# The table of the first two batches in another order: v-weight conversions ahead of the first state

## The chip, the cores and the metric

The kernel runs on one core of a Trainium2 chip. The time is the device time of one execution in microseconds (us); the number that counts is the median over several runs. The engines are TensorE (PE; its weight loads PEld), VectorE (DVE), ScalarE (ACT), GpSimd (POOL) and SyncE (SP), which here issues every transfer between HBM and the on-chip memory SBUF. Matmul results lie in PSUM banks.

## What is computed

Eight batches of 576 positions go through an attention with decay (eight heads of 64) and then through a gated block with a spatial mixing. Cut to what matters:

```python
scores = (q @ k.T) / sqrt(64)                      # per batch and head
x = (scores * gamma[h] ** (i - j) for i >= j) @ v  # heads side by side: 512 wide
h = maximum(x @ w_in, 0)                           # 512 -> 1024
u, v = h[..., :512], h[..., 512:]
v_n = (v - mean(v)) / sqrt(var(v) + 1e-6)
v_s = w_spatial @ v_n + b_spatial[:, None]         # over the 576 positions
out = (u * v_s) @ w_out                            # 512 -> 512
```

All inputs and outputs are 32-bit floats. A product of two of them is made of three products of halves (a high part, rounded, and the low rest), so each weight is converted once into such a pair before its first use.

## The kernel before

Each batch's positions are four chunks of 128 and a tail of 64. The attention is computed with a running state: a chunk needs its scores within itself (`scores_chain`, line 625: products of q and k, then a mask on VectorE into tile at), the state's update (`state_chain`, line 631: products of the scaled k and of v into PSUM; then sh, a decay in dec, and the next state st), and a burst of products with the state and with v (`burst_chain`, line 648). In the burst a tiny copy on ScalarE (`turned`, line 538: r<-warm) stands between the two halves; at its end ScalarE casts the chunk's result into slot (high part) and VectorE subtracts (low part). Before the update, k is scaled by the decay terms (`prep_k`, line 464, eight steps on ScalarE or one on another engine).

Weights come as 64-bit words and are converted by `weight` (line 394) in seven steps: absolute value (ScalarE), a clamp, two to three bit operations (VectorE), a cast to the high part (ScalarE), and a subtraction for the low part. Kind 1 are the v halves of w_in, in four blocks; kind 0 the u halves; kind 2 is w_out. `spatial` (line 418) splits w_spatial. `v_chain` (line 682) makes and normalizes v, `vs_chain` and `g_chain` the spatial mixing, `gated_chain` the gate, `f_chain` and `product_chain` the output. From batch 2 on the products go by a scheme with fewer products, and the weights' sums for it are made in between (`made_weight`, line 336).

The order of all this is written out by hand. Each entry of the tables ORDER (line 43), STEADY and LAST names a generator and advances it by one step; all engines issue in the program's order:

```python
for name in order.split():
    ...
    chain = chains.get(name)
    if chain is None:
        chain = chains[name] = makers[head](*rest)
    next(chain)
```

ORDER covers batches 0 and 1 and the start of batch 2 and 3, once. STEADY then runs for batches 2 to 5, and LAST for 6 and 7. The letters: d loads a chunk (its q and k, its k in the other layout, its v), D a weight block, S w_spatial, T a tail, c the constants (c.a is fixed_terms). g are scores, p the state, b the burst, q and k the scalings; w is a weight's conversion (w.1.3.vp is v block 3 with the clamp on VectorE and the subtraction on GpSimd), s the spatial split, v the v chain, U, V, G, P the first batch's gate, y and X the later gate, A the made weights, F and W output products, R, K, Y, Z their operands. An entry z is one dummy product (`spin`, line 230) of 128x512 that reads a zeroed part of wsp and whose result nobody reads; there are 43. BANKS (line 151) says which of the four PSUM banks m0 to m3 each use of a bank takes, in the order of use.

Buffers are shared: chunks 2 and 3 of batch 0 are loaded into tiles that are later u and wout0 (in the profile u and lent_wout), the four v blocks and later w_spatial into the tile of slot1 (lent_slot), the other weights into raw. Helpers record every operation at line 204, so all rows of the profile have this line.

Of the kernel before, what the change touches and what calls it, by code (L numbers as in the profile page):

```python
# [18 lines left out]
P = 128  # L19
B, H, S, D = 8, 8, 576, 64  # L20
# [28 lines left out]
    z.34.1 z.35.1 w.1.0.vp z.18.1 w.1.3.vp b.0.1 S z.4.1 b.0.1 w.1.3.vp w.1.0.vp z.8.1 p.0.1.aa b.0.1 S w.1.3.vp
    w.1.0.vp b.0.1 w.1.2.pp z.31.1 b.0.1 z.9.1 w.1.3.vp z.29.1 c.t z.37.1 k.0.2.a q.0.2.p z.38.1 w.1.2.pp g.0.2  # L50
    b.0.1 d.1.0 z.6.1 w.1.1.vp w.1.2.pp z.7.1 p.0.1.aa d.1.0 p.0.2.aa z.0.1 w.0.0.vp p.0.2.aa z.12.1 v.0.0 w.1.3.vp
    w.1.2.pp w.0.0.vp p.0.2.aa z.14.1 w.1.2.pp g.0.2 b.0.2 w.0.0.vp z.36.1 w.1.3.vp S v.0.1 w.0.1.vp p.0.2.aa
    w.1.3.vp w.0.0.vp v.0.0 k.0.3.a S w.0.1.vp v.0.0 m w.0.0.vp v.0.0 w.0.1.vp D.2.0 q.0.3.p b.0.2 v.0.0 d.1.0
    p.0.2.aa d.1.1 v.0.0 t.0.p t.0.p b.0.2 b.0.2 g.0.3 S w.0.2.pp p.0.3.ap w.0.1.vp s.1.p t.0.p z.28.1 w.0.2.pp
    p.0.3.ap v.0.1 b.0.2 g.0.3 p.0.3.ap v.0.1 b.0.2 q.1.0.p v.0.1 d.1.1 s.0.p p.0.3.ap s.1.p w.0.2.pp b.0.3 d.1.1
    g.1.0 w.0.1.vp b.0.3 v.0.1 b.0.3 k.1.0.p g.1.0 v.0.0 v.0.2 v.0.0 s.2.p v.0.2 s.0.p v.0.1 s.3.p b.0.3 w.0.0.vp
    w.0.2.pp s.2.p p.1.0.pp e.0.v T.1 v.0.0 v.0.2 e.0.v D.2.1 w.0.2.pp b.0.3 d.1.2 s.3.p v.0.2 v.0.1 D.0.3 b.0.3
    v.0.3 d.1.2 v.0.0 v.0.2 w.0.0.vp v.0.3 p.1.0.pp v.0.1 v.0.4 s.4.p v.0.2 v.0.4 p.1.0.pp w.0.2.pp v.0.4 k.1.1.p
    e.0.v v.0.3 v.0.1 v.0.2 v.0.1 b.1.0 s.4.p v.0.3 b.1.0 p.1.0.pp v.0.2 v.0.4 v.0.3 q.1.1.p U.1 v.0.4 w.0.1.vp
    v.0.4 s.5.p p.1.0.pp v.0.3 g.1.1 v.0.4 s.5.p b.1.0 U.1 b.1.0 v.0.4 d.1.3 v.0.2 p.1.1.pp d.1.2 v.0.2 U.0 w.0.1.vp  # L60
    b.1.0 v.0.4 p.1.1.pp b.1.0 p.1.1.pp v.0.4 V.0.0 w.0.2.pp U.0 V.0.0 v.0.3 g.1.1 V.0.0 v.1.0 v.0.3 w.2.0.vv
    k.1.2.p v.0.4 v.1.0 p.1.1.pp w.2.0.vv v.0.4 t.1.p v.1.0 v.0.3 v.0.4 p.1.1.pp v.1.0 v.0.3 q.1.2.p b.1.1 w.2.0.vv
    g.1.2 b.1.1 w.2.1.vp p.1.2.pa w.2.0.vv d.2.0 v.1.0 b.1.1 b.1.1 d.1.3 w.2.1.vp w.0.3.pv w.2.0.vv d.2.0 V.0.0
# [971 lines left out]
```

## Time and profile before

| what | value |
|---|---|
| median of 3 runs | 509.9 us (509.21 to 511.1) |
| span of the profiled execution | 506.5 us |
| TensorE busy (matmuls) | 498.4 us, 98% |
| TensorE weight loads | 472.6 us, 93% |
| VectorE, ScalarE, GpSimd busy | 395.2, 259.3, 152.1 us |

The profiled execution is one run; what the runs' time has beyond its span lies around the program. A row of the timeline gives the start and the length of one or several equal instructions, in brackets how long the engine was idle ahead of it and what ended that. The windows give each engine's busy time in a stretch and, as PEclk, the share of TensorE's full clock that was granted in it. The chain that ended last goes from step to step back to what released it. Dummy products count as busy.

### The profile page before, as it was taken

The numbers are of one execution on the slowest core, as the hardware profiler recorded it, in microseconds if no ns is written. First come the engines' busy times: TensorE is split into PE (matmuls) and PEld (weight loads), VectorE is DVE, ScalarE is ACT, GpSimd is POOL, SyncE is SP. The second block draws the span as 40 slices with busy tenths as digits, with TensorE's granted clock in tenths as the row PEclk, the third lists the DMA queues.
The fourth block names the chain that finished last, engine by engine and source line by source line (L and its number), as shares of the span: only waits on it lengthen the run. The fifth ranks groups of instructions, "written<-read, shape, count | busy, mean of one in ns | idle before, by whom it ended". The sixth has DMA issues, their size and how long they took to land.

```text
span 506.5 us, 17036 instructions
## 1 busy us (share of the span) xinstructions
PE 498.4 (98%) x7335; PEld 472.6 (93%) x7335; DVE 395.2 (78%) x881; ACT 259.3 (51%) x587; POOL 152.1 (30%) x133
## 2 busy tenths in 40 slices
PE   7999999999999999999999999999999999999997
PEld 5778999999999999999999999999999999999996
DVE  3798898768789886788669786888867886788756
ACT  2798544645344652537336472446525574357513
POOL 1499633314127430345014250243303240020000
PEclk8999999999999999999999999999999999999999
DMA  8987522025515422152222441054221520011002
GB/s 295 407 294 243 167 74 82 2 68 146 167 55 167 158 65 84 45 187 85 63 85 90 143 148 62 24 152 161 67 86 45 182 90 1 1 41 54 2 1 93
DMA packets 29516, 55.52 MB, mean 110 GB/s; under 512 B 2945, under 2 KB 15361, under 8 KB 29186
## 3 DMA queue, kind: packets, MB, share of 16 engines
q1 hardware_dynamic: 29442, 54.45, 32.8%
q8 instruction: 57, 0.93, 0.8%
q14 instruction: 17, 0.14, 0.1%
HBM read 45.00 MB, written 9.44 MB: 107 GB/s over the span
## 4 chain that ended last, share of the span: by engine, by line
PE 91%; DVE 4%; ACT 2%; DMA 1%; issue 0%; SPq 0%; DVEq 0%; ACTq 0%
PE m L204 78%; PE r L204 14%; DVE u L204 2%; DMA fixed_terms<-in_terms 1%; DVE slot L204 1%; ACT slot L204 1%; DVE kn L204 1%; ACT dec L204 0%; ACT u L204 0%; ACT lent_wout L204 0%; DVE x L204 0%; ACT f L204 0%; ACT win L204 0%; DVE at L204 0%; SPq L204 0%
## 5 line engine op out<-in xcount | busy, mean ns | idle before, releaser
L204 PE MATMUL m<-wsp,vn 128*128 128x288 f32 x768 | 113.0, 296 | 0.0
L204 PEld LDWEIGHTS m<-wsp,vn 128*128 128x128 f32 x768 | 105.1, 188 | 0.6
L204 DVE TENSOR_TENSOR u<-m,u 128x288 f32<-128x288 f32 (+1 forms) x132 | 57.2, 439 | 19.1 <-PE m L204 11.6
L204 ACT COPY u<-m 128x288 f32<-128x288 f32 (+1 forms) x92 | 34.5, 384 | 38.3 <-PE m L204 30.1
L204 PE MATMUL m<-slot,win 128*128 128x288 f32 x336 | 50.5, 296 | 0.0
L204 PEld LDWEIGHTS m<-slot,win 128*128 128x128 f32 x336 | 46.5, 188 | 0.6
L204 POOL TENSOR_TENSOR slot<-u,slot 128x576 fp32r<-128x576 f32 x7 | 10.2, 1463 | 105.4 <-ACT slot L204 105.4
L204 DVE SCALAR_TENSOR_TENSOR u<-u,m 128x288 f32<-128x288 f32 x48 | 21.2, 450 | 24.8 <-PE m L204 24.6
L204 PE MATMUL m<-slot,wout 128*128 128x288 f32 x264 | 39.5, 295 | 0.4 <-issue 0.4
L204 PEld LDWEIGHTS m<-slot,wout 128*128 128x128 f32 x264 | 36.5, 188 | 0.8 <-issue 0.5
L204 PE MATMUL m<-win,slot 128*128 128x512 f32 (+1 forms) x168 | 35.3, 348 | 0.0
L204 ACT CAST slot<-u 128x576 fp32r<-128x576 f32 x32 | 21.4, 675 | 24.1 <-DVE u L204 23.8
L204 PEld LDWEIGHTS m<-win,slot 128*128 128x128 f32 x168 | 27.1, 188 | 4.2 <-DVE slot L204 0.2
L204 ACT CAST places<-u 128x576 fp32r<-128x576 f32 x21 | 14.2, 677 | 32.1 <-DVE u L204 31.8
L204 PE MATMUL m<-quarter,slot 128*128 128x256 f32 x216 | 29.7, 283 | 0.0
L204 ACT COPY r<-warm 1x2 f32<-1x2 f32 x32 | 4.9, 152 | 48.3 <-PE r L204 47.5
L204 DVE TENSOR_TENSOR at<-r,fixed_terms 128x512 f32<-128x512 f32 x32 | 21.8, 682 | 7.7 <-DMA fixed_terms<-in_terms 4.9
L204 PE MATMUL m<-slot,part 128*128 128x288 f32 x168 | 27.1, 300 | 0.4
L204 PE MATMUL m<-wtl,vt 128*128 128x288 f32 (+1 forms) x128 | 27.4, 295 | 0.0
L204 PEld LDWEIGHTS m<-quarter,slot 128*128 128x128 f32 x216 | 26.9, 188 | 0.4
L204 POOL TENSOR_TENSOR kn<-kn,fixed_terms 128x512 f32<-128x512 f32 x15 | 15.7, 1044 | 38.5 <-DMA kn<-in_qkv 29.6
L204 PE MATMUL m<-places,wout 128*128 128x288 f32 x168 | 26.8, 297 | 0.0
(166 smaller groups left out, 1210.4 us busy)
## 6 DMA issues: line engine op xcount, KB each, us to landing
qk<-in_qkv SPq DMA_DIRECT2D x30, 512.0 KB, 4.2
kn<-in_qkv SPq DMA_DIRECT2D x30, 256.0 KB, 5.0
vv<-in_qkv SPq DMA_DIRECT2D x30, 256.0 KB, 4.7
out<-u SPq DMA_DIRECT2D x28, 144.0 KB, 1.8
tail<-in_tails SPq DMA_DIRECT2D x8, 384.0 KB, 3.7
out<-o SPq DMA_DIRECT2D x18, 144.0 KB, 1.9
lent_slot<-in_w_in SPq DMA_DIRECT2D x4, 512.0 KB, 7.9
raw<-in_w_in SPq DMA_DIRECT2D x4, 512.0 KB, 10.3
```

The lines of the kernel that those rows point to most:

```text
L204: ins = op(*args, **kw)
```

## The change

Only the table ORDER and the list BANKS that goes with it are new. ORDER has the same 726 entries as before, each as often, in another order; LAST is wrapped otherwise and holds the same entries; STEADY is untouched. BANKS has other digits throughout. The head of the table:

```diff
 ORDER = """
-    d.0.0 z.40.1 c.a z.22.1 d.0.0 z.17.1 d.0.0 z.10.1 D.1.1 d.0.1 z.16.1 d.0.1 z.24.1 d.0.1 z.13.1 z.15.1 D.1.0
-    z.39.1 g.0.0 D.1.2 g.0.0 q.0.0.p D.1.3 k.0.0.v d.0.2 p.0.0.va z.19.1 p.0.0.va z.26.1 D.0.1 z.23.1 w.1.1.vp
+    c.a d.0.0 q.0.0.p d.0.0 k.0.0.v z.31.1 z.30.1 D.1.1 d.0.0 w.1.1.vp w.1.1.vp w.1.1.vp w.1.1.vp w.1.1.vp z.18.1
+    z.20.1 z.0.1 z.41.1 z.42.1 z.3.1 z.6.1 z.39.1 z.22.1 z.28.1 z.2.1 z.38.1 z.40.1 z.21.1 z.5.1 z.10.1 D.1.0 d.0.1
...
```

At the start of VectorE's program stands, before, the first chunk's mask (at), the scaling of k (kn), the decay (dec) of the state, then the conversion of the first v block (lent_vn, with its PSUM bank m) with the state's sum (st) inside:

```order
L204 TENSOR_TENSOR at_135<-r_91,fixed_terms 128x512
L204 TENSOR_TENSOR kn_95<-kn_95,fixed_terms 128x512
L204 TENSOR_TENSOR dec_79<-sh,fixed_terms 128x256
L204 TENSOR_SCALAR lent_vn_92<-lent_vn_92 128x512
L204 TENSOR_SCALAR m_87<-lent_vn_92 128x512
L204 TENSOR_TENSOR st_76<-r_91,dec_79 128x256
L204 SCALAR_TENSOR_TENSOR m_87<-lent_slot_93,m_87 128x512
L204 SCALAR_TENSOR_TENSOR lent_vn_92<-lent_slot_93,m_87 128x512
```

and now:

```order
L204 TENSOR_TENSOR kn_96<-kn_96,fixed_terms 128x512
L204 TENSOR_SCALAR lent_vn_92<-lent_vn_92 128x512
L204 TENSOR_SCALAR m_88<-lent_vn_92 128x512
L204 SCALAR_TENSOR_TENSOR m_88<-lent_slot_93,m_88 128x512
L204 SCALAR_TENSOR_TENSOR lent_vn_92<-lent_slot_93,m_88 128x512
L204 TENSOR_TENSOR at_182<-r_91,fixed_terms 128x512
L204 TENSOR_TENSOR dec_79<-sh,fixed_terms 128x256
L204 TENSOR_TENSOR st_76<-r_91,dec_79 128x256
```

The scaling of k now comes first, then four steps of the v block, and only then the mask, the decay and the state's sum.

On ScalarE, from the burst of chunk 1 to the scaling of chunk 3's k (in lent_wout), stands before (u is chunk 2's k, slot the cast of a chunk's result, win a weight's cast, f a weight's absolute value):

```order
L204 COPY r_90<-warm 1x2
L204 CAST win_66<-lent_vn_92 128x512
L204 CAST slot_217<-r_90 128x2x4x64
L204 ACTIVATE u<-u,fixed_terms 128x64 x8
L204 ACTIVATE dec_78<-st_75,fixed_terms 128x64 x4
L204 ACTIVATE f<-raw 128x512
L204 CAST win_66<-lent_vn_92 128x512
L204 ACTIVATE dec_79<-sh,fixed_terms 128x64 x4
L204 CAST win_66<-lent_vn_92 128x512
L204 ACTIVATE f<-raw 128x512
L204 ACTIVATE lent_wout_197<-lent_wout_197,fixed_terms 128x64 x8
```

and now:

```order
L204 ACTIVATE lent_vn_92<-lent_slot_93 128x512
L204 ACTIVATE dec_78<-st_75,fixed_terms 128x64 x4
L204 ACTIVATE u<-u,fixed_terms 128x64 x8
L204 CAST win_66<-lent_vn_92 128x512
L204 ACTIVATE f<-raw 128x512
L204 COPY r_90<-warm 1x2
L204 CAST win_66<-lent_vn_92 128x512
L204 ACTIVATE f<-raw 128x512
L204 CAST slot_242<-r_90 128x2x4x64
L204 ACTIVATE dec_79<-sh,fixed_terms 128x64 x4
L204 ACTIVATE lent_wout_403<-lent_wout_403,fixed_terms 128x64 x8
```

Chunk 2's scaling moved ahead of the burst's little copy, of two weight steps and of the cast of chunk 1's result; the absolute value of the last v block and a decay went ahead of it.

On TensorE, from chunk 0's update (vv_96,kn_95) to chunk 1's (vv_108,kn_107), stands before, with dummies (m<-wsp), the two halves of the burst (qsc, at) and chunk 1's scores (qk):

```order
L204 MATMUL r_91<-vv_96,kn_95 64x64 x16
L204 MATMUL m_87<-wsp_68 128x512
L204 MATMUL m_88<-wsp_68 128x512
L204 MATMUL m_89<-wsp_68 128x512
L204 MATMUL r_90<-qsc_137,sh 64x64 x4
L204 MATMUL m_86<-wsp_68 128x512
L204 MATMUL r_90<-qsc_137,sh 64x64 x4
L204 MATMUL r_90<-at_135,vv_96 64x64 x16
L204 MATMUL r_91<-qk_106 64x64 x16
L204 MATMUL m_88<-wsp_68 128x512
L204 MATMUL m_89<-wsp_68 128x512
L204 MATMUL r_91<-vv_108,kn_107 64x64 x16
```

and now, from the last but one of eighteen dummies:

```order
L204 MATMUL m_87<-wsp_68 128x512
L204 MATMUL m_89<-wsp_68 128x512
L204 MATMUL r_91<-vv_97,kn_96 64x64 x16
L204 MATMUL r_91<-qk_95 64x64 x16
L204 MATMUL r_90<-qsc_99,sh 64x64 x8
L204 MATMUL r_91<-qk_129 64x64 x16
L204 MATMUL r_90<-at_182,vv_97 64x64 x16
L204 MATMUL r_91<-vv_131,kn_130 64x64 x16
L204 MATMUL m_86<-wsp_68 128x512
L204 MATMUL m_87<-wsp_68 128x512
```

The update stands ahead of chunk 0's scores (qk_95), the dummies between the products are gone, and 22 dummies follow behind chunk 1's update, where fourteen stood; two more stand behind the first three products of the v chain.

SyncE asks for fixed_terms first, for the first v block ahead of chunk 0's v, for the second ahead of chunk 1, and for all of w_spatial behind the q, k and v of batch 1's first chunk and the q and k of its second. Block 2 of the u weights is converted later, behind the work of batch 1's third chunk, and the first gated product is that of block 2 (G.0.2) instead of block 1. The last entries X of batch 1, the operands Y and Z behind them and the first output products W stand in another order.

## Rows read from the trace of the kernel before

**Rows 1.** The page's part 1: engine, busy us, share, count.
```profile
PE 498.4 (98%) x7335; PEld 472.6 (93%) x7335; DVE 395.2 (78%) x881; ACT 259.3 (51%) x587; POOL 152.1 (30%) x133
```

**Rows 2.** Windows: stretch, length, busy us by engine, clock, DMA share, GB/s.
```profile
5.00:10.00 5.00, 3.21 (x69) 2.15 (x67) 1.77 (x4) 1.05 (x2) 0.73 (x1) 0.80 1.01 365
10.00:15.00 5.00, 5.00 (x87) 3.52 (x86) 3.39 (x6) 1.95 (x7) 2.28 (x2) 0.51 1.07 431
15.00:20.00 5.00, 5.00 (x65) 3.71 (x64) 4.01 (x8) 3.33 (x10) 1.49 (x1) 1.00 1.03 393
30.00:40.00 10.00, 10.00 (x309) 8.29 (x301) 9.06 (x22) 9.00 (x24) 10.00 (x9) 1.00 0.82 240
60.00:165.00 105.00, 104.49 (x1587) 100.22 (x1586) 85.33 (x169) 51.51 (x121) 36.71 (x27) 1.00 0.33 102
165.00:506.00 341.00, 337.48 (x4737) 327.56 (x4735) 263.60 (x612) 167.00 (x363) 76.59 (x68) 1.00 0.26 82
```

**Rows 3.** Timeline, TensorE, 0 to 22 us: start, us, operation, [idle before].
```profile
1.50 3.77 PE L204 MATMUL m<-wsp 128*128 128x512 f32 x9 [1.50 <-DVE wsp L204]
...
15.61 3.51 PE L204 MATMUL m<-wsp 128*128 128x512 f32 x14
```

**Rows 4.** Chain that ended last, whole span: start us, us, engine and tile.
```profile
21.17 0.59 ACT slot L204
21.75 1.91 ACT u L204 x8
...
24.62 0.56 ACT f L204
25.19 0.51 ACT win L204
25.70 0.97 ACT dec L204 x4
...
27.75 1.91 ACT lent_wout L204 x8
29.66 0.05 ACT r L204
...
29.75 2.10 PE r L204 x128
...
148.53 0.36 issue
```

**Rows 5.** Timeline of DMA issues, then issues by window: KB each, us to landing.
```profile
2.58 0.63 SPq L204 DMA_DIRECT2D lent_slot<-in_w_in  x1
...
7.64 0.33 SPq L204 DMA_DIRECT2D u<-in_qkv  x1
...
11.22 3.07 SPq L204 DMA_DIRECT2D lent_wout<-in_qkv  x1
...
lent_slot<-in_w_in SPq DMA_DIRECT2D x1, 512.0 KB, 6.7
...
u<-in_qkv SPq DMA_DIRECT2D x1, 1024.0 KB, 11.7
...
lent_wout<-in_qkv SPq DMA_DIRECT2D x1, 1024.0 KB, 13.3
...
lent_slot<-in_w_sp SPq DMA_DIRECT2D x4, 288.0 KB, 7.2
```

**Rows 6.** Timeline, ScalarE, 7 to 30 us, with idle time ahead and its releaser.
```profile
21.17 0.59 ACT L204 CAST slot<-r 128x512 fp32r<-128x512 f32 x1 [0.88 <-PE r L204]
```

**Rows 7.** Timeline, VectorE, 11 to 25 us.
```profile
18.92 0.69 DVE L204 SCALAR_TENSOR_TENSOR lent_vn<-lent_slot,m 128x512 int32<-128x512 int32 x1
19.52 0.42 DVE L204 TENSOR_SCALAR lent_vn<-lent_vn 128x512 f32<-128x512 f32 x1
```

**Rows 8.** Window 28 to 56 us, GpSimd alone: length, busy us, clock, DMA.
```profile
28.00:56.00 28.00, 26.97 (x26) 1.00 0.69 216
```

**Rows 9.** Timeline, TensorE, 145 to 165 us.
```profile
162.99 0.69 PE L204 MATMUL r<-vv,kn 64*64 64x64 f32 x32 [0.15 <-DVE kn L204]
```

More of the change, by code (lines that the diff above doesn't have):

```diff
@@ L49 @@
[L49 to L63, printed above, removed]
@@ new lines @@
+    d.0.1 d.0.1 D.1.2 D.1.3 d.0.2 p.0.0.va g.0.0 p.0.0.va b.0.0 w.1.0.vp b.0.0 b.0.0 g.0.0 g.0.1 b.0.0 k.0.1.p
+    p.0.0.va p.0.0.va p.0.1.aa p.0.0.va w.1.0.vp w.1.0.vp p.0.1.aa b.0.0 w.1.2.pp z.1.1 z.17.1 z.33.1 z.36.1 z.24.1
+    z.16.1 z.35.1 z.4.1 z.11.1 z.7.1 z.14.1 z.9.1 z.27.1 z.15.1 z.37.1 z.23.1 z.12.1 z.25.1 q.0.1.p w.1.2.pp
+    w.1.0.vp w.1.0.vp b.0.0 p.0.1.aa p.0.1.aa w.1.0.vp w.1.1.vp w.1.3.vp p.0.1.aa w.1.0.vp m q.0.2.p w.1.1.vp
+    w.1.2.pp g.0.1 w.1.2.pp w.1.2.pp k.0.2.a D.0.1 D.0.0 z.13.1 z.8.1 z.34.1 z.32.1 v.0.0 z.29.1 z.19.1 b.0.1
@@ new lines @@
+    w.2.2.vv G.0.3 G.1.3 e.1.v G.0.3 P.0.0.p P.0.1.p v.1.1 w.2.3.vp w.2.3.vp w.2.3.vp w.2.3.vp G.1.3 v.1.2 v.1.2
+    v.1.2 v.1.2 w.2.3.vp v.1.2 v.1.1 v.1.4 v.1.4 v.1.4 P.0.1.p P.0.0.p w.2.1.vp v.1.4 F.0.0.1 k.2.1.a A.0.12.v
+    A.0.4.v e.1.v v.1.1 v.1.2 A.0.11.v A.1.0.v p.2.0.vp v.1.2 P.1.0.v v.1.2 w.2.2.vv F.0.0.0 d.2.1 b.2.0 p.2.1.vv
+    b.2.0 F.0.0.0 F.0.0.1 v.1.4 b.2.0 b.2.0 P.1.1.v v.1.3 v.1.3 v.1.3 v.1.3 y.1.2.1 v.1.2 p.2.0.vp p.2.1.vv
+    p.2.1.vv A.0.13.v v.1.4 v.1.2 A.0.14 A.0.15.v A.1.5.p w.2.3.vp v.1.4 v.1.4 P.1.1.v v.1.3 A.1.1.v A.1.2.p
@@ L93 @@
+    K.2.7.pv q.3.0.p K.2.6.vp W.1.2.0.B W.1.2.0.B W.1.2.1.E K.2.4.vp W.1.2.1.B W.1.2.1.B K.2.4.vp K.2.5.vp
+    W.1.2.1.B p.3.0.pv p.3.0.pv K.2.5.vp W.1.2.1.B W.1.2.0.E K.2.7.pv W.1.2.0.B W.1.2.1.E K.2.4.vp
 """
@@ new lines @@
+    K.b.5.vv X.a.1.0 X.a.1.1 W.a.1.1.E Y.a.1.v K.b.7.vv X.a.1.3 X.a.1.0 X.a.0.2 X.a.1.2 X.a.1.3 Z.a.5.vv Z.a.5.vv
+    X.a.0.3 X.a.1.2 Y.a.3.v Z.a.7.vv Y.a.3.v Z.a.7.vv W.a.2.1.A X.a.0.3 Z.a.6.vv Y.a.2.v W.a.2.0.A Z.a.7.vv
+    W.a.2.0.D W.a.2.0.A Y.a.2.v W.a.2.1.A W.a.2.1.D W.a.2.0.D Z.a.5.vv W.a.2.0.C W.a.2.1.D Z.a.6.vv W.a.2.1.C
+    W.a.2.0.C R.b.2.v Z.a.6.vv W.a.2.0.B W.a.2.1.C W.a.2.0.A Z.a.4.vv W.a.2.1.A Z.a.4.vv W.a.2.0.A R.b.2.v
+    W.a.2.1.B W.a.2.1.A W.a.2.0.A Z.a.4.vv R.b.3.p W.a.2.1.A R.b.3.p W.a.2.0.A W.a.2.0.B W.a.2.1.E W.a.2.1.A
@@ new lines @@
+    W.a.2.0.B W.a.2.0.B K.b.7.vv W.a.2.1.B W.a.2.0.E K.b.6.pv W.a.2.1.B W.a.2.1.B W.b.0.0.C W.a.2.0.E W.a.2.1.E
+    W.b.0.0.A K.b.6.pv K.b.7.vv W.a.2.1.E W.a.2.0.B W.b.0.1.A K.b.6.pv W.b.0.0.A W.a.2.0.E W.b.0.0.C W.b.0.1.C
+    W.a.2.1.C W.b.0.1.A K.b.4.vv K.b.5.vv W.a.2.1.B W.b.0.0.A W.a.2.0.C K.b.5.vv W.b.0.1.A W.b.0.0.A W.b.0.1.C
+    K.b.4.vv W.b.0.0.A K.b.4.vv W.b.0.0.B W.b.0.0.A W.b.0.1.A W.b.0.0.E W.b.0.0.B W.b.0.0.B W.b.0.0.E v.b.0.v
+    W.b.0.1.E W.b.0.0.B v.b.0.v W.b.0.1.A v.b.2.a W.b.0.1.B v.b.2.a v.b.0.v v.b.4 v.b.0.v W.b.0.1.A v.b.4 v.b.2.a
@@ new lines @@
+    Y.b.2.v X.b.1.0 X.b.1.3 Y.b.2.v X.b.1.2 X.b.1.0 X.b.0.1 X.b.1.2 Y.b.3.v X.b.0.0 X.b.0.1 Y.b.3.v W.b.1.1.B
+    X.b.0.0 Y.b.1.v X.b.1.1 Y.b.1.v W.b.1.1.B W.b.2.1.C X.b.1.1 Z.b.5.vv W.b.2.1.D Z.b.7.vv Z.b.5.vv W.b.2.1.A
+    W.b.2.1.D Z.b.6.vv W.b.2.0.D W.b.2.1.A W.b.2.1.C Z.b.6.vv W.b.2.0.C Z.b.4.vv W.b.2.1.C Z.b.7.vv W.b.2.0.A
+    Z.b.6.vv Z.b.7.vv W.b.2.1.A W.b.2.0.A Z.b.4.vv Z.b.5.vv W.b.2.0.A W.b.2.0.D W.b.2.1.A W.b.2.1.B W.b.2.0.C
+    W.b.2.0.A W.b.2.0.C W.b.2.1.A Z.b.4.vv W.b.2.0.A W.b.2.1.A W.b.2.1.B W.b.2.0.B W.b.2.0.A W.b.2.1.B W.b.2.1.B
```

104 lines of the change are left out of this document (46 added, 58 removed).

## The prediction

> **What bounds the kernel now.** I read the page's busy line first, then the windows, the chain that ended last, and the timelines of the first 30 us. The busy line calls TensorE busy for 98% of the span [rows 1], and the windows show it without a hole from 30 us on: 10.00 of 10 us, then 104.49 of 105, then 337.48 of 341 [rows 2]. So after about 30 us the time is matmul work alone, which this change leaves as it is, and a gain or loss can come only from where that stream begins and from waits that the new table makes inside the 165 us that it covers. In the first 30 us busy does not mean useful. 43 dummy products (the z entries) stand there, which read the zeroed wsp tile. The first nine take 3.77 us, 0.42 each, and fourteen later ones 3.51 us, 0.25 each [rows 3]: these are the two levels of TensorE's clock, 1.2 and 2.4 GHz. The granted clock fell to 0.80 and 0.51 in the windows from 5 and 10 us [rows 2], after TensorE had waited for the first chunk; from 15 us it is full.
>
> What the dummies cover is seen in the chain: from 21.2 us to 29.7 us it lies on ScalarE, not on TensorE. Two steps of eight scalings mark it, those of chunk 2's k (tile u, 1.91 us from 21.75) and of chunk 3's k (tile lent_wout, 1.91 us from 27.75), and then TensorE goes on at 29.75 with chunk 3 [rows 4]. From there the chain is TensorE's. The load of chunk 2 was issued at 7.64 and took 11.7 us, so it lay ready at 19.3 us; that of chunk 3, issued at 11.22 with 13.3 us, at 24.5 us [rows 5]. ScalarE came to the first 2.4 us after its landing, since the cast of chunk 1's result stands ahead of it, waited 0.88 us for TensorE, and began only at 21.17 [rows 6]. **The stage to cost is ScalarE's row of work from about 19 us to chunk 3's scaling.**
>
> **The change, part by part.** No instruction is added or taken out; every entry of the table appears as often as before, and the steady rounds and the last one have the same entries. My sum follows one milestone: the end of chunk 3's scaling, after which TensorE goes on with chunk 3. By counting the products in both orders, the same real work stands ahead of that milestone in each, so the same is left behind it.
>
> *Loads.* The fixed terms go first, the first v-weight block ahead of chunk 0's v, the second ahead of chunk 1. Chunk 0's v now comes as the fifth of the same five transfers of which that block was the last before, and the block landed at 2.58 + 6.7 = 9.3 us [rows 5]. So v lands near 9.3 us, and the block one v load earlier: 256 KB at the 365 GB/s of the window from 5 us [rows 2] are 0.7 us, which gives 8.6 us (an estimate). Up to chunk 2's load the set is the same, so 19.3 us stays, and 24.5 us likewise.
>
> *Dummies ahead.* Eighteen stand in front instead of nine, from 1.50 us. At 0.25 to 0.42 each they end between 6.0 and 9.1 us. The state's first products can't begin before v at 9.3 us, so the dummies cost nothing there, and nine fewer stand behind.
>
> *Conversions in front of the state.* VectorE now scales kn and then works off four steps of block 1 before chunk 0's mask and decay. An instruction of 512 columns takes it 0.69 us, a clamp or a short sum 0.42 [rows 7]. With the block's absolute value taken on ScalarE up to 9.2 us, the four end near 11.7 and the state's first sum comes near 13 us. Queued behind are the mask, the decay and the sum on VectorE, chunk 1's decay on ScalarE, and chunk 1's update on TensorE, which comes near 14 us. All this is later than it could be without the conversions, but ScalarE's row below doesn't wait for it: it waits for chunk 2's landing. From 9.2 us to the last step of v-weight block 3, VectorE's list holds fifteen instructions of 512 columns and seven short ones, 15 x 0.69 + 7 x 0.42 = 13.3 us. They overlap a little and wait a little for ScalarE, so I take 22.6 us for the end.
>
> *ScalarE's row.* Chunk 2's scaling now stands ahead of the cast of chunk 1's result. Counting what is ahead of it, ScalarE is free at about 19.5 us, when the load has just landed. Then follow, with the shares of the chain as durations [rows 4]: scaling 1.91, cast of a weight 0.51, absolute value 0.56, the little copy 0.05, cast 0.51, absolute value 0.56, cast of the result 0.59, four decay steps 0.97, chunk 3's scaling 1.91; together 7.6 us, which ends at 27.1 us. The second weight cast waits for VectorE's 22.6 us, where ScalarE arrives at about the same time; I add 0.3 us for that and for the copy, which waits for TensorE: 27.4 us. Before, the step ended at 29.66 us. **Difference: 2.2 us earlier.** The bounds: chunk 3's load at 24.5 us plus 1.91 gives 26.4 us, 3.2 us earlier, and it can't be better. The other bound is the dummies behind chunk 1's update: 24 of them now lie between 14.6 us (the update's end) and the product that the little copy waits for. At 0.25 each that is 6 us and TensorE is there at about 22 us, with the copy due at 22.6; at 0.42 each it is 10 us, TensorE comes at about 25.5, and the row ends at 30.3 us, 0.7 us later than before. I take the fast value, since from 14.6 us TensorE has unbroken work, and after such work from about 11.5 us on the granted clock of before rose to 1.00 [rows 2].
>
> *Spatial weights and other later entries.* The w_sp loads now go behind the loads of batch 1's first two chunks. Their raw tile is free when VectorE has done block 3, at 22.6 us; with 7.2 us to landing [rows 5], and up to twice that behind the loads now ahead, they land between 30 and 37 us. By its list ScalarE comes to their first cast at about 36 us, and the first product that needs them now has three more real matmuls of 512 columns' worth ahead of it than before. I cost this at nothing; if the cover is gone it is at most 2 us. On GpSimd, busy 26.97 of the 28 us from 28 to 56 [rows 8], the work before block 2 of the u weights grows, since that block's low part moves behind batch 1's third and fourth chunk. Summing the durations of such rows along its new list, GpSimd delivers it near 61 us, and TensorE's first gated product, which now is that block's, would come at about 65 us (both are estimates): covered by 4 us.
>
> *Second half of the table.* The last sums of batch 1 are laid so that only one quarter hangs on the last two of them, and the first output product stands ahead of these. Before, TensorE waited 0.36 us at 148.5 and for scaled kn 0.15 us at 162.99 [rows 4, 9]. If both go, another 0.5 us; new waits there I bound at 0 to 1 us, and take zero for the sum of both.
>
> **Sum.** The profiled execution spans 506.5 us; the median of the three runs is 509.9 us, so 3.4 us lie around the span and stay. 506.5 - 2.2 = 504.3, and with 3.4: 507.7 us.
>
> **The rivals.** *More is gained.* ScalarE reaches chunk 3's scaling at its landing (3.2 us) and both late waits go (0.5 us): 509.9 - 3.7 = 506.2 us. For it: the waits are in the trace. Against: ScalarE's row has 7.6 us of work behind a landing at 19.3 us, so it would have to lose nothing anywhere.
>
> *The gain is lost to the clock.* TensorE has nothing to do between the end of its eighteen dummies and 9.3 us, and short products with waits up to 14 us. Before, a wait of that kind was followed by the 0.51 window. If the lower level lasts to beyond 20 us, the dummies take 0.42 each and the row ends 0.7 us later than before: 510.6 us. At half of that, 509.1 us. The Trainium skill (TensorE: Matmul & The Clock Gate, Part 1: The HAM clock gate) says that the throttled level is the default and that only sustained activity releases it, and (Why this matters for your kernels) warns of idle gaps between bursts; by it the wait at 7 to 9 us speaks against this change. The trace agrees as far as the fall after 5 us goes; whether the new gap does the same no run yet shows.
>
> *Slower: GpSimd becomes the bound between 30 and 65 us.* Its clamp of u block 2 waits for ScalarE's absolute value, which now stands behind batch 0's last chunk, and behind that clamp wait batch 1's q, the four spatial weights, and finally that block's low part. The cover is 4 us and the gain ahead of it 2.2 us, so from 6.2 us of additional delay on the kernel is slower than before. Rows on GpSimd take up to 1.5 us each, and some eighteen stand between; should each wait a further 0.5 us for decay sums, it is 9 us late, so 509.9 + 9 - 6.2 = 512.7 us. For it: the 96% load. Against: the same engine has only 36.71 of 105 us of work after 60 us [rows 2], and its list is no longer than before.
>
> *Nothing changes.* If TensorE's stream is held from elsewhere (VectorE was busy 9.06 of 10 us from 30 to 40), the head start melts away: 509.9 us.
>
> **How the numbers follow.** Forecast, a gain of 1.3 to 3 us: 0.48. More gained: 0.14. Lost to the clock or elsewhere, within 1.3 us of before: 0.21. Slower by GpSimd or another late order of the half that I can't cost row by row: 0.17. A measurement of this kernel tells apart about 0.5%, 2.55 us. Faster by more than that (below 507.35) is the rival of more gain and a good third of the forecast: 0.32. Slower by more (above 512.45): 0.15. Within: 0.53. The range reaches from 505.9, the best bound with 0.3 us for the spread, to 512.3 us, which leaves out most of the slower case.
>
> **What would show it.** Right: chunk 3's eight scalings on ScalarE end at 27 to 28 us, TensorE's last dummy starts near 32 us with three more v products' worth done than before, the first state update starts near 9.3 us, and chunk 2's scaling directly at its landing. The windows after 30 us stay full. Wrong: a granted clock below 1 after 16 us (the clock rival), a wait of TensorE or a pause before a gated product at 55 to 70 us with GpSimd named (the slower one), w_sp landing after 38 us, or late waits on VectorE between 100 and 165 us larger than 0.5 us in all.

## The result, and the profile after

The changed kernel takes 512.29 us (median of 7 runs, 511.26 to 514.04), the kernel before 508.7 us (7 runs): a ratio of 1.0058, with a 95% interval of 1.0033 to 1.0083, so some 3 us slower. A second set of runs, below, gives 1.0079 (1.0054 to 1.0103). The forecast was 507.7 us. Time and span of one execution lie 1.8 us apart (514.04 and 512.2 us for the one profiled); the 3.4 us of the prediction had taken the difference between one execution and the median of others into it, and the median of before that it started from was 1.2 us above that of the seven runs.

Part 1 of the page and the windows that answer to [rows 1, 2] (the columns are the same):

```profile
PE 499.6 (98%) x7335; PEld 476.0 (93%) x7335; DVE 403.3 (79%) x881; ACT 260.5 (51%) x587; POOL 153.3 (30%) x133
```

```profile
5.00:10.00 5.00, 3.87 (x23) 2.76 (x24) 0.95 (x2) 0.66 (x1) 0.73 (x1) 1.00 1.01 384
10.00:15.00 5.00, 3.73 (x172) 3.25 (x171) 4.38 (x9) 1.87 (x7) 2.12 (x2) 0.94 1.03 396
15.00:20.00 5.00, 5.00 (x31) 3.99 (x25) 4.71 (x9) 4.91 (x15) 3.98 (x5) 0.72 1.05 397
30.00:40.00 10.00, 7.75 (x267) 6.61 (x258) 7.72 (x21) 7.29 (x21) 5.69 (x5) 0.91 0.53 167
60.00:165.00 105.00, 103.93 (x1565) 99.20 (x1563) 92.20 (x171) 52.08 (x118) 36.65 (x28) 1.00 0.27 87
165.00:506.00 341.00, 339.41 (x4841) 329.52 (x4840) 266.07 (x613) 167.78 (x366) 80.52 (x70) 1.00 0.26 82
```

Before, 10.00 of the 10 us from 30 us were busy; now it is 7.75, with a granted clock of 0.91. From 60 to 165 us, 103.93 us are busy instead of 104.49. In this trace the low clock that before showed from 8 to 15 us comes later and is shorter (0.94 and 0.72 in the windows from 10 and 15 us). The clock's record begins at 7.6 us here and at 4.6 us in before, and a window without a record shows 1.00; the first dummies, 0.43 us each up to then, tell of the lower level.

The dummies and the places where TensorE stood, from its timeline (answering to [rows 3, 9]; in brackets the idle time ahead and what ended it):

```profile
1.50 7.18 PE L204 MATMUL m<-wsp 128*128 128x512 f32 x18 [1.50 <-DVE wsp L204]
```

```profile
15.33 6.41 PE L204 MATMUL m<-wsp 128*128 128x512 f32 x22
...
34.91 0.30 PE L204 MATMUL r<-at,lent_wout 64*64 64x64 f32 x8
37.46 0.58 PE L204 MATMUL r<-at,lent_wout 64*64 64x64 f32 x24 [2.25 <-issue]
...
38.09 0.93 PE L204 MATMUL r<-qk 64*64 64x64 f32 x32
```

```profile
161.15 2.78 PE L204 MATMUL m<-win,places 128*128 128x256 f32 x22 [0.58 <-POOL places L204]
...
167.75 0.69 PE L204 MATMUL r<-vv,kn 64*64 64x64 f32 x32 [1.17 <-DVE kn L204]
```

There are three waits of note: 2.25 us at 35.2 us in the midst of a group of 32 equal products, with no engine named ("issue"), 0.58 us at 160.6 for GpSimd (tile places), and 1.17 us at 166.6 for VectorE (tile kn), where before had 0.15 us.

ScalarE's row, whose end was the milestone of the forecast, and VectorE ahead of it (timelines, answering to [rows 6, 7]):

```profile
20.16 2.02 ACT L204 ACTIVATE u<-u,fixed_terms 128x64 f32<-128x64 f32 x8
...
24.35 0.62 ACT L204 CAST win<-lent_vn 128x512 fp32r<-128x512 f32 x1 [0.84 <-DVE lent_vn L204]
...
26.90 2.00 ACT L204 ACTIVATE lent_wout<-lent_wout,fixed_terms 128x64 f32<-128x64 f32 x8
```

```profile
20.66 1.48 DVE L204 TENSOR_SCALAR lent_vn<-lent_vn 128x512 f32<-128x512 f32 x1
...
23.63 0.69 DVE L204 SCALAR_TENSOR_TENSOR lent_vn<-lent_slot,m 128x512 int32<-128x512 int32 x1
```

Chunk 3's scaling (lent_wout) ends at 28.9 us. It ended at 29.7 before, so it is 0.8 us earlier and not 2.2. Even these 0.8 us can't be credited to the new order. How long TensorE's low clock stretch (1.2 GHz) behind the first dummies lasts differs between executions, and the milestone goes with it. The runs named here are described below; pl_before and pl_after are the two kernels with their buffers at other addresses, late_dec has the new front unchanged. The rows are ScalarE's of pl_after, then pl_before:

```profile
27.60 2.02 ACT L204 ACTIVATE lent_wout<-lent_wout,fixed_terms 128x64 f32<-128x64 f32 x8
```

```profile
25.95 2.05 ACT L204 ACTIVATE lent_wout<-lent_wout,fixed_terms 128x64 f32<-128x64 f32 x8
```

| low clock after the first dummies | old order: scaling ends at | new order (14 traces that start as the changed kernel does) |
|---|---|---|
| 6.8 us | 29.7 (before), 29.5 (r_before) | 29.6 (pl_after), 29.5, 30.3 |
| 3.4 us | | 28.9 (after), 29.2 (r_after), five more from 28.5 to 29.1 |
| none | 28.0 (pl_before) | 28.3 (late_dec), 28.9, 29.3, 29.3 |

By these traces, with a low stretch of the same length the new order reaches the milestone at most 0.2 us earlier, and with none it is later.

**How far the work is.** To see where time goes when the order differs, I price each real product (dummies left out) with the mean distance of its shape in the steady rounds of before (0.232 us for 512 columns, 0.136 for 288, 0.121 for 256, 0.0166 for 64x64), sum along each trace, and compare the times at which equal work is done. Positive means later than in the trace of before; the heading is the time there.

| trace | 28.7 | 35.3 | 42.0 | 67.4 | 97.4 | 122.2 | 154.4 | 173.0 | 453.1 us |
|---|---|---|---|---|---|---|---|---|---|
| after | -1.4 | -0.6 | +2.7 | +2.1 | +2.7 | +3.2 | +2.7 | +4.8 | +5.7 |
| after, second (r_after) | -1.1 | -0.3 | +1.2 | +0.7 | +1.5 | +2.1 | +1.6 | +3.8 | +4.7 |
| before, second (r_before) | -0.1 | +0.1 | +0.6 | +0.6 | +0.6 | +0.6 | +1.2 | +1.2 | +1.4 |

So there is a head start of about 1 us at 28.7 us, which by the table above is in good part the clock's (in pl_after, with a low stretch as long as before's, it is 0.5 us; pl_before is 1.7 us ahead in the old order). It turns into a loss between 35 and 42 us, some more goes up to 122 us, 2 us go between 154 and 173 us, and another 0.9 us from 173 us on, where both kernels issue the same products in the same order.

### The profile page after: what moved, and what is told of

Its sections match the earlier page's. It is cut to its first block, busy times and chain, and to the rows that moved or that the text cites. A ratio compares the mean times of both kernels' runs of the same rounds, so it can differ in the third digit from the quotient of the medians.

```text
span 512.2 us, 17020 instructions
## 1 busy us (share of the span) xinstructions
PE 499.6 (98%) x7335; PEld 476.0 (93%) x7335; DVE 403.3 (79%) x881; ACT 260.5 (51%) x587; POOL 153.3 (30%) x133
## 4 chain that ended last, share of the span: by engine, by line
PE 76%; DVE 15%; DMA 2%; issue 2%; ACT 2%; POOL 1%; SPq 1%; DVEq 0%; POOLq 0%
PE m L204 65%; PE r L204 11%; DVE u L204 3%; DMA kn<-in_qkv 2%; DVE slot L204 2%; DVE x L204 1%; DVE m L204 1%; DVE room L204 1%; DVE quarter L204 1%; SPq L204 1%; DVE lent_vn L204 1%; ACT slot L204 1%; DVE kn L204 1%; DVE places L204 1%; DVE at L204 0%
## 5 line engine op out<-in xcount | busy, mean ns | idle before, releaser
L204 ACT COPY u<-m 128x288 f32<-128x288 f32 (+1 forms) x92 | 34.4, 383 | 36.8 <-PE m L204 29.6
L204 PE MATMUL m<-win,slot 128*128 128x512 f32 (+1 forms) x168 | 35.8, 353 | 0.2 <-DVE slot L204 0.2
L204 ACT CAST places<-u 128x576 fp32r<-128x576 f32 x21 | 14.2, 676 | 32.8 <-DVE u L204 31.0
L204 POOL TENSOR_TENSOR kn<-kn,fixed_terms 128x512 f32<-128x512 f32 x15 | 15.9, 1061 | 37.5 <-DMA kn<-in_qkv 37.5
L204 POOL TENSOR_TENSOR places<-x,places 128x576 fp32r<-128x576 f32 x6 | 10.6, 1765 | 55.2 <-ACT places L204 55.2
```

The lines of the kernel that those rows point to most:

```text
L204: ins = op(*args, **kw)
```

## Which stretch of the table loses

Three kernels take the first part of the new table and the rest in the order of before. All kernels of this group ran on one chip beside before (508.74 us).

```diff
-ORDER = the 726 entries as changed
+ORDER = the first 154 (or 322, or 550) entries as changed, then the others in the order of before
```

> The first 154 entries of the table as changed (up to the burst of chunk 2, some 29 us), the rest in the order of before. Theory one, the front is a small gain: in the trace of the changed kernel the real matmul work stood 0.45 us ahead at 30 us, so about 508.3 us against the 508.7 of before. Rival, the front itself is the loss (conversions ahead of the state): 510 us or more, with waits of TensorE between 27 and 35 us.

Measured: 510.87 us, ratio 1.0049 (1.0035 to 1.0064). That looks like the rival, but the trace says otherwise: the work is 1.4 us ahead at 28.7 us and falls behind at 33.9 us, by a wait that belongs to the seam. The loads of w_spatial come late, as in the new table, while the casts of w_spatial stand early, as in the old one:

```profile
32.90 0.67 ACT L204 CAST wsp<-lent_slot 128x576 fp32r<-128x576 f32 x1 [2.24 <-DMA lent_slot<-in_w_sp]
33.48 0.58 ACT L204 CAST slot<-r 128x512 fp32r<-128x512 f32 x1
```

```profile
34.92 0.24 PE L204 MATMUL r<-qsc,sh 64*64 64x64 f32 x1 [1.02 <-DVE slot L204]
```

ScalarE waits 2.24 us for the load, chunk 2's cast (slot) stands behind it, and TensorE waits 1.02 us for that. The run tells nothing against the front; it shows that these casts and loads had to move together.

> The first 322 entries as changed (up to the burst of batch 1's second chunk, some 68 us), the rest as before. The trace of the changed kernel has a pause of TensorE of 2.25 us at 35.2 us, in the midst of a group of 64x64 products, with no engine named and a fetch of instructions beginning at 35.07 us; then the granted clock is low once more. If that pause belongs to this order it recurs here and costs 2.3 to 3.3 us: 510.5 to 512 us. If it was of that one execution only: 508 to 509 us.

Measured: 514.22 us, ratio 1.0118 (1.0089 to 1.0147), above both forecasts. The pause is not in its profiled execution (0.36 us between two products there, and -0.8 us at 40 us in the sum of the table above), but the seam brings a wait of 1.75 us at 67.9 us. As a price of the first 322 entries the run is worthless.

> The first 550 entries as changed (some 130 us), the rest as before. Theory: against the run with 322 entries only the short waits at 99 and 113 us are new, 0.5 to 0.7 us more than that one. If the loss lies in the middle of the table (GpSimd between 30 and 130 us), it is here and not in the run with 322: 2 us more than that one.

> The changed kernel once more. 512.3 us. Its waits at 160 to 167 us (0.58 and 1.17 us in the trace, GpSimd and VectorE named) should be 2 us more than in the run with 550 entries if the end of the table is a part of the loss; if the pause at 35 us recurs in this execution, within 1 us of the same place, it is no accident of one run.

Measured: h_a550 511.29 us, 1.0060 (1.0042 to 1.0078), against the theory 2.9 us less than h_a322, which has the wait at its seam; r_after 512.37 us, 1.0079 (1.0054 to 1.0103). The two intervals overlap, so the times alone don't show the end of the table as a loss. The traces do: from 154 to 173 us r_after loses 2.2 us and the other traces of the new end lose 1.8 to 2.2, while h_a550, with the old end, loses none (+3.3 and +3.3), and the five other kernels that join the new start to the old end lose 0.1 us at most. The pause came back in both at the same product, 1.98 us in r_after. The list BANKS goes with the order in all these kernels and wasn't tried alone.

## The addresses

Behind 173 us the same products come in the same order, and yet the changed kernel loses 0.9 us there, evenly. Product by product, those of vn with wsp are 0.8 ns further apart, those of places with win 2.7 ns. The order of the table also decides in which order buffers are first used, and so where they lie in SBUF.

```diff
+    for name, shape, dtype, tag in (
+        ("lent_vn0", [128, 4, 512], F32, "vn0"),
...
+    ):
+        keep(name, shape, dtype, tag)
```

> The kernel before, with its buffers laid out in SBUF as in the changed kernel (the buffers are taken once at the start in the other kernel's order of first use; no instruction is changed or moved). Behind 173 us both kernels issue the same products in the same order, yet in two traces of the changed kernel they come 0.96 us later at the end than at 173 us: 0.8 ns more for each product of vn with wsp, 2.7 ns for each of places with win. If the addresses do that: 509.5 to 509.9 us against 508.7, with the drift in the trace. If it is something else in the table: 508.7 us, no drift.

> The changed kernel with the buffers laid out as before. If the addresses make the drift: 511.3 us against 512.3, and the products behind 173 us as long as before. Otherwise 512.3 us.

Measured: pl_before 510.31 us, 1.0027 (1.0010 to 1.0044), where nothing but addresses differs from before; pl_after 511.57 us, 1.0053 (1.0036 to 1.0070). That new addresses slow the old order is clear of the noise; that the old ones speed up the new order isn't by the times, since this interval overlaps those of the changed kernel. In the traces pl_after loses 0.0 us from 173 to 453 us (+3.5 and +3.5), pl_before 1.8 us (+0.6 and +2.4), of which 0.8 us is in the two groups of products; what the rest is stays open. The groups (TensorE, busy us and mean ns of one) of before, after, pl_before and pl_after in turn:

```profile
L204 PE MATMUL m<-wsp,vn 128*128 128x288 f32 x768 | 113.0, 296 | 0.0
```

```profile
L204 PE MATMUL m<-wsp,vn 128*128 128x288 f32 x768 | 113.6, 297 | 0.0
```

```profile
L204 PE MATMUL m<-wsp,vn 128*128 128x288 f32 x768 | 113.9, 297 | 0.4 <-issue 0.4
```

```profile
L204 PE MATMUL m<-wsp,vn 128*128 128x288 f32 x768 | 112.9, 296 | 0.0
```

The means follow the layout (296 ns with that of before, 297 with the new one), not the table. Over all twenty traces these products, from 173 to 453 us, are either 133.3 to 133.4 or 134.1 to 134.2 ns apart, the first in every trace with the old layout. Which buffer's address does it wasn't tried; vn1 for one lies 64 bytes lower (185,440 instead of 185,504).

## The pause at 35 us

I took the pause for a lack of instructions. The instruction queue q8 brings 57 blocks of 16 KB in the execution, for 14,747 rows of TensorE (matmuls, weight loads, and those of its sequencer), some 259 each. In the trace TensorE's pause stands at its row 1217, and a block of q8 begins at 35.07 us, 2.4 us ahead of the first product behind it. The DMA view from 30.3 to 35.0 us and from 34.5 to 36.5 us (queue and kind: packets, MB, share):

```profile
q1 hardware_dynamic: 638, 1.23, 75.3%
q14 instruction: 2, 0.02, 0.9%
```

```profile
q1 hardware_dynamic: 61, 0.11, 16.1%
q8 instruction: 1, 0.02, 3.0%
```

From 30.3 to 35.0 us no block of TensorE's comes, and then one does. That stretch is full of data: 1.23 MB.

First I moved long products ahead of the pause:

```diff
-    g.1.0 g.1.0 v.0.1 b.0.3 b.0.3 k.1.0.p
+    g.1.0 g.1.0 v.0.1 b.0.3 v.0.2 v.0.2 v.0.2 v.0.2 b.0.3 k.1.0.p
```

> The changed kernel with four steps of the third v product (v.0.2, twelve products of 512 columns, 2.8 us) moved ahead of the last half of chunk 3's burst (b.0.3), that is, ahead of the place where TensorE paused. Theory: TensorE paused at its row 1217, the same in every trace, since the block of instructions behind it had not come; its fetch began at 35.0 us and the rows went on 2.4 us after. With the long products ahead, TensorE is busy until the block is there: pause under 0.3 us, no second fall of the granted clock, 509.4 to 510.4 us. Rival, TensorE waited for data there (a wait that the profile doesn't name): the pause stays at that product, 512.3 us.

Measured: 514.97 us, 1.0114 (1.0089 to 1.0139), against the theory. The pause is gone from its trace, but TensorE then stands 1.9 us at 40 us, for the tail's cast: the twelve products had covered that. At 42 us the work is 1.4 us behind, as in r_after. And since the fetch began at 33.3 us in this execution, the run doesn't tell the theories apart.

```diff
-        for part in parts:
-            part()
+        for i, part in enumerate(parts):
+            if (b, c) != (1, 1) or i == 2:
+                part()
```

> The changed kernel without two loads, the q, k block (512 KB) and the second k block (256 KB) of batch 1's second chunk; that chunk then computes with old data. Theory: the fetch waits behind the data that SyncE has put in the queues, so with 768 KB fewer it starts 1 to 2 us earlier (33 to 34 us) and the pause at row 1217 falls below 1 us: 510 to 511 us. Rival, the fetch is asked for late by TensorE itself: it starts at 35.0 us again and the pause stays at 2 us.

Measured: the fetch starts at 31.6 us, there is no pause, and the work stays 1.1 us ahead to 67 us and more, as the theory had it. The time, 512.8 us (1.0078; 1.0047 to 1.0109), did not follow: the runs go from 510.3 to 515.0, the profiled one took 511.5. So the pause isn't all of the loss: without it this trace is 1.2 us ahead at 67 us and yet 3.2 us behind at 453 us, by short waits (1.3 us up to 122 us), the late waits (2.1 us) and the stretch behind 173 us (1.1 us).

Next, the same bytes in another order:

```diff
-    T.0 d.1.0 c.t D.0.2 d.1.0 d.1.1 d.1.0
...
-    S S S S d.1.1 S d.1.2 v.0.1
+    T.0 d.1.0 c.t d.1.0 d.1.1 d.1.0
...
+    S S S S d.1.1 S D.0.2 d.1.2 v.0.1
```

> The changed kernel with the 512 KB of u-weight block 2 (D.0.2) asked for behind w_spatial, and that block's first two steps later. The same bytes are loaded, 512 KB fewer of them ahead of the fetch of instructions that came at 35.0 us. Theory: the fetch starts 1 to 2 us earlier, the pause at row 1217 falls to under 1 us, and the real work stands 1 us or more further at 40 us than in the changed kernel: 510.8 to 511.6 us. Rival: pause of 2 us as before, 512.3 us.

> As d02_late, but the steps of u-weight block 2 stand behind the tail's cast and chunk 3's low part, so that no engine's row waits for the late load (in d02_late VectorE stood 6.6 us behind it). Theory: the fetch of instructions starts near 33 us instead of 35, the pause at row 1217 is under 1.2 us, and at 42 us the real work stands where before had it or up to 1 us further (the changed kernel: 1.2 us behind): 510.8 to 511.5 us. Rival, the pause was not what cost: 512.3 us again.

Measured: d02_late 519.73 us, against the theory; the fetch starts at 33.0 us and the pause is 0.97 us, but VectorE waits 6.6 us behind the late load, and TensorE 5.6 us for VectorE. In d02_b that wait is gone, yet its fetch started at 34.7 us and the pause was 2.25 us: 513.55 us, 1.0098 (1.0068 to 1.0127), against the theory. best550b and best250b, below, have the same first 250 entries as d02_b: in the one the fetch started at 31.1 us and there was no pause, in the other at 34.8 us with a pause of 1.70 us. So the start of the fetch differs by 3.7 us between executions of the same entries, and loading those 512 KB later doesn't set it.

That left the first question, whether the pause hangs on the row count at all. Some short dummies at the very start shift the count and nothing else:

```diff
             pe.matmul(ps, idle[:, :P], idle, start=True, stop=True)
+        for i in range(20 if name == "idle31" else 0):
+            pe.matmul(ps[:, :64], idle[:, :P], idle[:, :64], start=True, stop=True)
```

> The changed kernel with 20 short dummy products of 64 columns (40 rows of TensorE) behind the very first dummy, where TensorE has nothing to do. Theory: the pause is at a row count, the end of a block of instructions: it stays at row 1217 and so lies 40 rows earlier in the program, ahead of the first product of at with lent_wout (in the state's part of the burst) instead of behind the eighth, if in this execution the fetch starts after 34 us. Rival, TensorE waits for data there: the pause stays behind the eighth product, at row 1257.

> The same with 8 short dummies (16 rows): pause at row 1217, that is, right ahead of the first product of at with lent_wout; rival: behind the eighth, at row 1233.

> The kernel before once more. Its trace had a step of 0.19 us at row 1217, which TensorE reached at 37.26 us, 2.2 us after the fetch began at 35.07. Theory: again no pause over 0.5 us there unless the fetch starts after 35.3 us; row 1217 between 36.5 and 38 us, 508.5 us.

Measured, one execution each: more20 515.21, more8 513.01, r_before 509.77 us. In more20 TensorE reached row 1217 only at 36.5 us, after a fetch at 32.8 us, and went on without a pause, so that its theory wasn't tested there. more8 and r_before did pause, and at that row (TensorE's timelines of more8, then r_before):

```profile
35.07 0.30 PE L204 MATMUL r<-qsct,st 64*64 64x64 f32 x8
35.55 0.69 PE L204 MATMUL r<-at,lent_wout 64*64 64x64 f32 x32 [0.19 <-issue]
```

```profile
35.75 1.66 PE L204 MATMUL m<-win,slot 128*128 128x512 f32 x6
...
38.04 0.63 PE L204 MATMUL r<-at,lent_wout 64*64 64x64 f32 x28 [0.44 <-issue]
```

In more8 the pause (0.19 us idle, 0.41 from product to product) stands ahead of the first product of at with lent_wout, where the changed kernel has it behind the eighth: 16 rows earlier in the program, and row 1217 again. In before the same row falls behind the first of them. A second row of this kind, 4801, lies 40 rows earlier in the program of more20 and so at another product (r<-att,tail instead of m<-slot,wout):

```profile
150.70 0.44 PE L204 MATMUL r<-att,tail 64*64 64x64 f32 x10 [0.69 <-issue]
```

The steps over 0.55 us between TensorE's products from row 1000 on, in all twenty traces:

| steps at row 1217 + 256 k | seen in |
|---|---|
| 1217 | after, r_after, h_a550, pl_after, pl_before, late_dec, d02_late, d02_b, best250b, r_before |
| 1473, 1729, 2497, 4289 | more20; late_dec; early_v, more8 and more20; pl_before |
| 4801 | before, r_before, h_a322, h_a550, pl_before, best550, best250b, more8, more20 |

These rows are exact multiples of 256 apart, in programs in which they hold different products. The steps at other rows stand before products that wait for a named engine, but for five of 0.59 us at rows 1430 and 1454, which have no idle time in them and lie in a low clock stretch. Below row 1000 it is the same: TensorE stands at row 705 in ten traces (0.24 to 1.31 us) and at row 961 in three (0.36 to 1.12 us), all with the new start, as in more8:

```profile
30.60 0.21 PE L204 MATMUL r<-qsc,sh 64*64 64x64 f32 x1 [1.12 <-issue]
```

All 41 idle times of TensorE over 0.15 us that the twenty profiles put down to "issue" lie at such a row. The pause of before at 148.5 us that [rows 4] shows as "issue" is one of them. That TensorE lacks its next block there is shown. In the ten traces with a pause at row 1217, and in more8, it went on 2.3 to 2.8 us after the fetch had begun; five of them, and two without a pause:

| trace | fetch begins, us | TensorE reaches row 1217 | goes on |
|---|---|---|---|
| r_before | 35.5 | 37.6 | 38.0 |
| after | 35.1 | 35.2 | 37.5 |
| r_after | 34.9 | 35.6 | 37.6 |
| d02_late | 33.0 | 34.8 | 35.8 |
| no_d11, best550b | 31.6, 31.1 | 35.2, 34.8 | no pause |

This is the fourth fetch. Its place in the count is 256 rows before the pause, at row 961, which TensorE reached at 30.5 us in the trace of the changed kernel; the fetch began 4.6 us later. In the ten traces with the pause it began 2.9 to 4.6 us after its place, in those without it 0.8 to 2.4 us, but for h_a154 (3.6 us) and before (3.9 us), where TensorE came to row 1217 later. From 60 us on, where fewer data move, most blocks begin between 1.7 us ahead of their place and 1.7 us behind it, 0.6 us behind in the middle. What sets the start of the fetch, 31.1 to 35.5 us in the traces above, stays open.

## The headline edit alone

```diff
-    D.1.1 d.0.0 w.1.1.vp w.1.1.vp w.1.1.vp w.1.1.vp w.1.1.vp z.18.1
+    D.1.1 d.0.0 w.1.1.vp z.18.1
...
-    p.0.0.va p.0.0.va p.0.1.aa
+    p.0.0.va p.0.0.va w.1.1.vp w.1.1.vp w.1.1.vp w.1.1.vp p.0.1.aa
```

> The changed kernel with four steps of v-weight block 1 (clamp and three bit operations) put back behind chunk 0's mask, decay and state sum on VectorE. Theory: they cost nothing where they stand, since ScalarE's row waits for chunk 2's landing (20.1 us) and then for VectorE's whole list: the state's first sum comes 2 us earlier (near 11.7 us), chunk 3's scaling still ends at 28.9 us within 0.5, 512.3 us within 0.8. Rival, the conversions in front hold the state up and are the loss: 510 to 511 us.

Measured: 513.07 us, 1.0079 (1.0057 to 1.0100). The time lies in the range of the theory, but neither mechanism came out. The state's first sum comes at 13.8 us, as in after, since it waits for ScalarE's copy and for TensorE; VectorE idles in that time, and the four steps now stand behind. Chunk 2's scaling starts at 22.6 instead of 20.2 us and chunk 3's ends at 31.5:

```profile
22.59 2.01 ACT L204 ACTIVATE u<-u,fixed_terms 128x64 f32<-128x64 f32 x8
...
29.54 2.01 ACT L204 ACTIVATE lent_wout<-lent_wout,fixed_terms 128x64 f32<-128x64 f32 x8
```

So the conversions ahead of the state fill idle time of VectorE. At this milestone they bring 2.6 us against after, and 1.9 us against pl_after, whose low clock stretch is as long as this one's (6.8 us). But at 42 us the two kernels stand alike (+1.1 and +1.2): this one reaches row 1217 at 37.4 us, without a pause, where the changed kernel waits until 37.5.

## The end of the table

```diff
-    K.2.5.vp K.2.7.pv p.3.0.pv R.2.2.p W.1.2.0.E
+    K.2.5.vp K.2.7.pv R.2.2.p p.3.0.pv W.1.2.0.E
```

> The changed kernel with one step moved near 158 us: on GpSimd the low part of a quarter of x (R.2.2, tile places) goes ahead of a decay (p.3.0) that stands between it and its sum. Theory: GpSimd's row is the cause of the two waits at 160 and 167 us; the part is ready 1.1 us earlier, the wait of 0.58 us at 160 us goes, that of 1.17 us at 167 us shrinks by half: 511.3 us against 512.3. Rival, the waits come from VectorE's own row: 512.3 us.

Measured: 513.37 us, 1.0082 (1.0057 to 1.0108). The wait for places at 160 us went, as the theory said; two short ones (0.15 and 0.27 us) came for it, and the wait for kn stayed at 1.17 us, so from 154 to 173 us the loss is 2.1 us as before the edit. The rival is right: VectorE's own row ends it. Its last two steps there, in the changed kernel, and what GpSimd does meanwhile (their timelines):

```profile
147.42 0.68 DVE L204 TENSOR_TENSOR kn<-kn,fixed_terms 128x512 f32<-128x512 f32 x1
...
163.91 1.97 DVE L204 TENSOR_TENSOR slot<-x,slot 128x576 fp32r<-128x576 f32 x1
165.80 1.89 DVE L204 TENSOR_TENSOR kn<-kn,fixed_terms 128x512 f32<-128x512 f32 x1
```

```profile
161.75 5.39 POOL L204 TENSOR_TENSOR slot<-x,slot 128x576 fp32r<-128x576 f32 x3
```

The last of these three by itself:

```profile
165.22 1.92 POOL L204 TENSOR_TENSOR slot<-x,slot 128x576 fp32r<-128x576 f32 x1
```

The scaling of kn takes 1.89 us beside GpSimd's subtractions, 0.68 us at 147.4 us without them. It ends 0.55 us after the end of the subtraction that was under way when it began (167.14 us), and in six other traces 0.54 to 0.55 us after it likewise: its time is what is left of GpSimd's instruction and 0.55 us more. Before has the same pair at the same price (1.62 and 1.90 us, from 159.5 us); there the row began early enough to cost TensorE 0.15 us. Which of the moved entries delays that row by about a microsecond stays open; that it is the entries from 550 on is shown by the trace of h_a550.

## A version without the losses

```diff
-ORDER = the 726 entries as changed
+ORDER = the first 550 (or 250) entries of d02_late or d02_b, then the others in the order of before
+    the buffers taken in the order of before
```

> What the runs so far point to in one kernel: the first 550 entries as changed, with u-weight block 2 loaded late as in the run d02_late, the rest of the table in the order of before, and the buffers laid out as before. If the three losses add up (the end of the table 1.1 us, the addresses 0.7 us, the pause about 1 us), 512.3 - 2.8 = 509.5 us; if the pause goes as a whole, 508.5 us; below 508 us only if the head start of 0.9 us at 30 us lasts as well.

> The first 550 entries of d02_b, then the order of before, buffers laid out as before. The end of the table and the addresses gave back 1.1 and 0.7 us each alone, the pause 1 us or more: 509 to 509.5 us; waits at 99 and 113 us (0.9 us in the changed kernel) are still in it.

> The same with the first 250 entries only (some 52 us), so that the waits at 99 and 113 us are out as well: 508 to 508.6 us, 0 to 0.7 us faster than before, if the seam between the two orders brings no wait; each wait that it brings shows in the trace between 52 and 90 us.

Measured: best550 517.17 us, spoilt by the same late load as d02_late; best550b 510.88 us, 1.0050 (1.0033 to 1.0067); best250b 513.51 us, 1.0091 (1.0063 to 1.0119), with the pause (1.7 us) and a wait at its seam. All three missed their forecasts. The median of best550b is 1.4 us below the changed kernel's 512.3, but the intervals overlap, so the return isn't shown by the times; it is still slower than before. Its trace has no pause and is 1.6 us ahead at 42 us. At 42.4 us TensorE waits 1.1 us for VectorE, which had waited 1.1 us for GpSimd's clamp of the late block, and the waits near 98 and 113 us are in it too. Behind 173 us it loses another 1.5 us, 1.1 of them in one wait for GpSimd (tile kn) at 291.9 us. No kernel here beats before, so how the loss divides among its causes is read from traces and not confirmed by a time.

## Why the prediction was wrong, step by step

- **"After about 30 us the time is matmul work alone"** is the step that failed. It had [rows 2, 4] for it, in which TensorE is full, and the unnamed 0.36 us at 148.5 us against it. Between 30 and 40 us before was already close to a second bound: it reached row 1217 of TensorE at 37.3 us and had its next block at 37.5. The new order reaches the same row up to 2 us earlier and, where the fetch comes late, has to wait for the same moment. And it has less done by then: 24 products of 512 columns stand ahead of that row instead of 30, 6 x 0.23 = 1.4 us. In the traces with the long pause this is the swing from a head start to a loss of 1.2 us (r_after); in the first trace the granted clock fell once more after the pause and took another 1.4 us. The pause is one part of the loss: the trace of no_d11 hasn't got it and still ends 3.2 us behind, by the waits and the stretch behind 173 us that the points below name.
- **The milestone**, "2.2 us earlier", failed as a term of the sum: 27.4 us was forecast, 28.9 came, and at a low clock stretch as long as before's it was 29.6 us, no earlier than in before (29.5 to 29.7). The 0.8 us of the first trace are luck of the clock. Chunk 2 landed at 20.1 us and not 19.3 (its load was issued at 9.04 instead of 7.64), and VectorE's last step of block 3 ended at 24.3 us instead of 22.6. Its list was as counted, fifteen long rows and seven short ones; but it began at 9.7 instead of 9.2 us, waited twice for TensorE (0.75 us), and a clamp of 0.42 us took 1.48 beside GpSimd's scaling of q. ScalarE waited 0.84 us for the end of it, where before had no wait from chunk 2's scaling on. That the conversions belong in front is right within the new order (undo_front); that the new order is ahead there isn't shown.
- **"I take zero"** for the second half of the table. The two late waits of before didn't go; they became 0.58 and 1.17 us, 2 us in all between 154 and 173 us. Short waits from 80 to 122 us took another 0.9. I had bounded new waits at 1 us.
- **Not in the sum at all**: the addresses, 0.9 us in the trace, and by the times of pl_before 0.5 to 2.2 us.
- **The clock rival** is not what lost the time, but the clock mattered more than I gave it: after the gap of 1.1 us ahead of 9.8 us the low stretch was 3.4 us in after and r_after and 6.8 us in pl_after, as in before; late_dec and pl_before had none. So it differs between executions and not by the order, and with it the milestone moves, by 1.7 us in the old order (before and pl_before) and by 1.3 us in the new one (pl_after and late_dec). The Trainium skill (TensorE: Matmul & The Clock Gate, Why this matters for your kernels), by which the prediction let that gap speak against the change, warns of longer gaps than this one.
- **The rival of GpSimd** from 30 to 65 us gave nearly the measured time, for a reason that didn't occur: no wait for GpSimd stands there in the trace, w_spatial landed by 36.8 us, and the first gated product wasn't late.
- The range ended at 512.3 us, the measured median; the chance of 0.15 for slower was too low for what was left uncosted: an order of 726 entries of which I followed one row.

## What to carry to other kernels

Where the profile names no engine for a pause ("issue"), count TensorE's rows: if such pauses lie whole blocks of 256 rows apart, instructions are a resource with its own due times, and putting many short products early brings the next block's due time forward. A gain ahead of such a point is worth only what the point lets through. Before an order is credited or blamed, hold the buffers' addresses fixed, look at a stretch in which both programs are the same, and compare traces whose low clock stretches are equally long.
